# The product of attention weights and v: f32 exponentials as moving operand for even heads, f16 pairs for odd heads

## The chip, the cores and the metric

One core of one Trainium2 chip runs the whole program in one launch. The metric is the device time in microseconds (us), the median of several runs. Engines are named as the profile names them: PE (TensorE matmuls), PEld (its weight loads), DVE (VectorE), ACT (ScalarE), POOL (GpSimd), SP (the engine whose queue issues the loads here).

## The reference, cut to what matters

```python
# q, k, v: (2, 8, 768, 64) f32; centroids: (8, 16, 64)
q_assign = argmax(einsum('bhsd,hcd->bhsc', q_n, c_n)); k_assign likewise
mask   = q_assign[:, :, :, None] == k_assign[:, :, None, :]
scores = where(mask, q @ k.T / 8, -1e9);  scores -= max(scores)
attn   = exp(scores);  attn = attn / (sum(attn) + 1e-9)
x      = (attn @ v)                   # the product that is changed
x      = moe(x)                       # x @ w_in, an activation, @ w_out
out    = moe2(x)                      # 8 experts, Sinkhorn-balanced gates
```

There are 16 heads (2 x 8) of 768 queries, 768 keys and 64 columns of v. A query whose cluster holds no key has all its scores at -1e9, so its row is the mean of all v; the kernel calls this case "absorbed" by the tables `Wt`.

## The kernel before, in words

Everything that must be exact to f32 is done on PE with f16 pairs: a value is split into a high f16 part and the f16 rest, and a product takes three matmuls (high x high, high x rest, rest x high), each at the f16 pace.

Attention (L395 to L975) is a hand-written software pipeline. A **unit** is one head and one tile of 128 keys, so a head has `NJ` = 6 units, the stage has `NU` = 96, and a pair of heads, which shares its preparation, has 12. The loop at L952 counts steps `g`; in step `g` the engines' queues get, in this order:

- `max_unit` for unit `g + 8` (L659): two matmuls of 384 columns into `pmt`, the one PSUM tile of its kind, and one DVE reduction of 768 columns (L675) that finds the row maxima. The next `max_unit` can only write `pmt` when this reduction is done.
- `e_split` for unit `g - 1` (L732): the exponentials `E`, f32, are cast to `Eh` (f16) on ACT (L740), or on DVE (L738) for 3 units of 12; then POOL forms the rest `El = E - Eh` in two halves of 384 columns (L742).
- `s_mm` for unit `g` (L711): four matmuls of 384 columns (L721, L725) give the scores of 128 keys against 768 queries, and one ACT instruction takes the exponentials of 768 columns (L729).
- `pv_mm` for unit `g - LAG`, `LAG` = 4 (L745): `Eh` and `El` are the stationary operands, six tiles of 128 queries each, and v the moving one, 64 or 65 columns (the 65th is a column of ones that sums the weights). That is 6 x 2 matmuls with `Eh` (v's high and rest part) and 6 with `El`: 18 in a unit, and 12 more with `Wt` in the last unit of a head (L766 to L770). The result has queries on the partitions.
- the tasks that `PLACE`, `PLAN2`, `PLANV` (L470, L929, L930) and the loops at L940 to L951 give to this step, woven with a few DVE chains (`weave`, L695): the preparation of later pairs of heads (loads, scaling, f16 splits of q and k, cluster argmax, DMA transposes by SP), the f16 pair of v (`vhi` on ACT L522, `vlo` on DVE L527), the tables `Wt` (`abs1` on PE L613, `abs2` on DVE L623 to L641), the decoding of the first MoE weights (`w00`, L187 to L205, L380, L383), and the evacuation of finished heads (`evac_tasks`, L774: DVE L787 to L789, ACT L794, POOL L797, and for odd heads the DMA transposes into `xT` L800).

All engine queues are in order, so a step that waits holds up all behind it on its engine. PSUM has 8 banks: `pmt` takes 2, the score tiles `ps_s` 2 x 2, and `ps_v` (`pv`, `abs`, `sim`, `red`) 2. When the last units have run, PE goes on with the first MoE layer (`l1_mm`, L898), of which two groups are put among the last two attention steps.

Of the kernel before, what the change touches and what calls it, by code (L numbers as in the profile page):

```python
# [8 lines left out]
F32 = mybir.dt.float32  # L9
# [9 lines left out]
P = 128  # L19
# [12 lines left out]
def attention_moe_kernel(  # L32
# [39 lines left out]
    one = const.tile([P, 1], F32, name="one")  # L72

# [327 lines left out]
    ps_s = actx.enter_context(tc.tile_pool(name="ps_s", bufs=2, space=PSUM))  # L401
    ps_v = actx.enter_context(tc.tile_pool(name="ps_v", bufs=2, space=PSUM))
# [6 lines left out]
    Wt = [ap1.tile([P, 2, 130], F16, name=f"Wt{i}") for i in range(2)]  # L409
# [60 lines left out]
    PLACE = [-34, -31, -28, -28, -27, -26, -25, -25, -24, -24, -23, -19, -18, -17, -16, -15, -14, -14, -21, -19, -11, -9, -9]  # L470

    def prep_tasks(p, parts=None):
# [134 lines left out]
        def abs1():  # L607

            ps = ps_v.tile([P, 2, 256], F32, tag="v", name=f"abs{p}")
            for h in range(2):  # L610
                for j in range(NJ):
                    t = h * NJ + j
                    nc.tensor.matmul(  # L613
                        ps[:, h, 0:129], lhsT=ka[:, t, :], rhs=d["vn"][:, t, 0:129],
                        start=(j == 0), stop=(j == NJ - 1))
            d["ab"] = ps

        def abs2():
# [3 lines left out]

            def hi(h):  # L623
                nc.vector.tensor_scalar(
                    out=w[r, h, 0:D + 1], in0=ps[r, h, 0:D + 1], scalar1=c[r, h:h + 1], scalar2=None, op0=ALU.mult)

            def rest(h):
                nc.vector.scalar_tensor_tensor(
                    out=t[r, h], in0=ps[r, h, 0:D], scalar=c[r, h:h + 1], in1=w[r, h, 0:D],
                    op0=ALU.mult, op1=ALU.subtract)  # L630

            def lo(h):
                nc.vector.scalar_tensor_tensor(
                    out=w[r, h, D + 1:129], in0=ps[r, h, D + 1:129], scalar=c[r, h:h + 1], in1=t[r, h],
                    op0=ALU.mult, op1=ALU.add)
# [23 lines left out]
    def max_unit(i, j):  # L659
# [7 lines left out]
        ps = ps_s.tile([P, 2, 512], F32, tag="s", name=f"pm{i}_{j}") if early else pmt  # L667
# [41 lines left out]
    pvt = {}  # L709

    def s_mm(i, c):  # L711

        p, hh = divmod(i, 2)
        d = st[p]
        ps = ps_s.tile([P, 2, 512], F32, tag="s", name=f"pS{i}_{c}")
# [4 lines left out]
        for g in range(2):  # L720
            nc.tensor.matmul(  # L721
                ps[:, g, 0:N2], lhsT=d["kB"][:, t, :], rhs=qb[:, hh * S + g * N2:hh * S + (g + 1) * N2],
                start=True, stop=False)
        for g in range(2):
            nc.tensor.matmul(  # L725
                ps[:, g, 0:N2], lhsT=d["kA"][0:KR, t, :], rhs=qa[0:KR, g * N2:(g + 1) * N2],
                start=False, stop=True)
        E = ap2.tile([P, 2, N2], F32, tag="E", name=f"E{i}_{c}", bufs=3)
        nc.scalar.activation(E, ps[:, :, 0:N2], AF.Exp, scale=d["esc"][:, 0:1])  # L729
        EE[i, c] = E  # L730

    def e_split(i, c):  # L732
        E = EE.pop((i, c))
        Eh = ap3.tile([P, 2, N2], F16, tag="Eh", name=f"Eh{i}_{c}", bufs=5)
        El = ap3.tile([P, 2, N2], F16, tag="El", name=f"El{i}_{c}", bufs=5)
        n = NJ * i + c
        if n % 12 in (0, 3, 5) or n >= NU - LEAD and n % 2:
            nc.vector.tensor_copy(Eh, E)  # L738
        else:
            nc.scalar.copy(Eh, E)  # L740
        for g in range(2):
            nc.gpsimd.tensor_tensor(out=El[:, g], in0=E[:, g], in1=Eh[:, g], op=ALU.subtract)  # L742
        EE[i, c] = (Eh, El)
# [899 lines left out]
```

## Time and profile before

| | |
|---|---|
| median of 3 runs | 1530.16 us (1527.67 to 1531.33) |
| the profiled execution, span from first to last instruction | 1526.7 us |
| busy in the span: PE, PEld, DVE, ACT, POOL | 1418.7, 764.8, 955.4, 665.3, 387.8 us |
| mean granted PE clock | 0.974 of 2.4 GHz |
| attention's exponentials, first to last start | 39.5 to 288.7 us |
| last matmul of the product with v | 296.9 us |

The profiled execution gives its span alone; what lies around it (launch and end) is in the runs' times. The median is 3.5 us above this span. Attention is the first fifth of the program; behind it come the two MoE parts, in which PE is busy throughout. The change touches attention alone, so the rows below are almost all of this stage. A time per unit is a stretch's length by the number of its exponentials; a busy time by the same number is the work that an engine has per unit.

### The profile page before, as it was taken

What the parts mean: (1) busy time and instruction counts of PE and PEld (TensorE: products, weight loads), DVE (VectorE), ACT (ScalarE), POOL (GpSimd) and SP (SyncE); (2) the same over time, 40 slices, a digit from 0 to 9 for tenths busy, and PEclk for the clock granted to TensorE, in tenths of its full rate; (3) what the DMA queues carried; (4) which work ended last, traced back from release to release, by engine and by line L of the source; (5) the groups of instructions that cost most, each with busy time, mean ns of one, the idle gap of its engine ahead of it and who ended that gap; (6) DMA issues with size and microseconds to landing.
All of it is one profiled execution on the core that took longest, in us unless ns stands there. A gap on an engine that the chain in (4) does not pass through costs nothing.

```text
span 1526.7 us, 22967 instructions
## 1 busy us (share of the span) xinstructions
PE 1418.7 (93%) x9289; PEld 764.8 (50%) x9289; DVE 955.4 (63%) x1732; ACT 665.3 (44%) x1123; POOL 387.8 (25%) x427
## 2 busy tenths in 40 slices
PE   3878888898999998999999999999999999999998
PEld 1555556543444444544555555555555555555554
DVE  7889898876756866466565466466456565564333
ACT  2677777475553444343344333333333333324221
POOL 1579889752101321030030020020020020021000
PEclk9799899898999998999999999999999999999999
DMA  9675743331321100101101101101101101100011
GB/s 217 145 162 102 134 87 62 91 116 52 129 69 56 56 0 1 55 1 56 56 1 55 56 1 56 56 1 56 55 1 55 56 1 55 38 19 1 1 42 42
DMA packets 106633, 87.60 MB, mean 57 GB/s; under 512 B 78368, under 2 KB 88608, under 8 KB 106528
## 3 DMA queue, kind: packets, MB, share of 16 engines
q1 hardware_dynamic: 106528, 86.15, 20.8%
q8 instruction: 72, 1.18, 0.3%
q14 instruction: 33, 0.27, 0.1%
HBM read 64.01 MB, written 3.15 MB: 44 GB/s over the span
## 4 chain that ended last, share of the span: by engine, by line
PE 71%; DVE 17%; ACT 5%; issue 4%; DMA 1%; POOL 0%; DVEq 0%; ACTq 0%; POOLq 0%; SPq 0%
PE o L1471 11%; PE o L1472 11%; PE o L1470 11%; PE X L1521 5%; PE X L1524 5%; PE X L1523 5%; PE Y L1521 4%; PE Y L1524 4%; PE Y L1523 4%; DVE pmt L675 3%; PE l L1248 2%; PE pmt L672 1%; PE l L912 1%; PE l L913 1%; PE l L914 1%
## 5 line engine op out<-in xcount | busy, mean ns | idle before, releaser
L1472 PE MATMUL o<-w_s,hl 128*128 128x512 f16 x768 | 291.6, 380 | 0.0
L1471 PE MATMUL o<-w_s,hh 128*128 128x512 f16 x768 | 291.5, 380 | 0.0
L1470 PE MATMUL o<-w_s,hh 128*128 128x512 f16 x768 | 291.3, 379 | 0.0
L1540 ACT ACTIVATE hh<-u 128x384 f16<-128x384 f32 x192 | 100.3, 522 | 374.9 <-DVE u L1536 374.9
L742 POOL TENSOR_TENSOR El<-E,Eh 128x384 f16<-128x384 f32 x192 | 189.3, 1014 | 72.8 <-DVE Eh L738 41.2
L1541 DVE SCALAR_TENSOR_TENSOR hl<-u,hh 128x384 f16<-128x384 f32 x192 | 112.8, 587 | 120.1 <-ACT hh L1540 120.1
L1536 DVE TENSOR_TENSOR u<-X,snap 128x384 f32<-128x384 f32 x64 | 35.7, 557 | 189.5 <-PE X L1524 189.5
L121 POOL PARTITION_ALL_REDUCE w_m<-w_mx x14 | 5.4, 383 | 570.2 <-DVE w_mx L1336 332.7
L1523 PEld LDWEIGHTS <-wop 128*128 128x128 f16 x896 | 87.9, 98 | 93.6 <-issue 13.5
L1521 PEld LDWEIGHTS <-wop 128*128 128x128 f16 x896 | 87.9, 98 | 81.9 <-issue 1.1
L1536 DVE TENSOR_TENSOR u<-Y,snap 128x384 f32<-128x384 f32 x128 | 70.8, 553 | 80.1 <-PE Y L1524 79.1
L1472 PEld LDWEIGHTS <-hl 128*128 128x128 f16 x768 | 75.2, 98 | 90.8 <-issue 0.3
L1248 PE MATMUL l<-hh,w_s 128*128 128x512 f16 x384 | 118.3, 379 | 0.0
L1524 PEld LDWEIGHTS <-wop 128*128 128x128 f16 x896 | 87.9, 98 | 58.5 <-issue 0.9
L729 ACT ACTIVATE E<-pS,esc 128x768 f32<-128x768 f32 x96 | 86.2, 900 | 65.7 <-PE pS L725 48.4
L1470 PEld LDWEIGHTS <-hh 128*128 128x128 f16 x768 | 76.0, 99 | 66.5 <-issue 0.2
L1529 ACT COPY snap<-X 128x384 f32<-128x384 f32 x128 | 61.2, 478 | 109.7 <-PE X L1524 108.3
L1471 PEld LDWEIGHTS <-hh 128*128 128x128 f16 x768 | 75.2, 98 | 66.5 <-issue 0.2
L675 DVE TENSOR_REDUCE pmt<-pmt 128x1 f32<-128x768 f32 x84 | 80.6, 960 | 19.5 <-PE pmt L672 18.7
L672 PE MATMUL pmt<-kA,qA 80*128 80x384 f16 x184 | 52.1, 369 | 42.5 <-DVE pmt L675 14.2
L1248 PEld LDWEIGHTS <-w_s 128*128 128x128 f16 x576 | 56.4, 98 | 67.5
L1521 PE MATMUL X<-xop,wop 128*128 128x384 f16 x256 | 83.8, 327 | 6.8 <-ACT snap L1529 5.5
(280 smaller groups left out, 2990.5 us busy)
## 6 DMA issues: line engine op xcount, KB each, us to landing
w_raw<-in_moe_w_dram SPq DMA_DIRECT2D x16, 2048.0 KB, 8.2
w_c<-in_moe_w_out_dram SPq DMA_DIRECT2D x16, 512.0 KB, 3.5
w00x<-in_moe_w_in_dram SPq DMA_DIRECT2D x8, 512.0 KB, 5.6
w00f<-in_moe_w_in_dram SPq DMA_DIRECT2D x8, 512.0 KB, 4.1
w_c<-in_moe_w_in_dram SPq DMA_DIRECT2D x8, 512.0 KB, 3.8
qraw<-in_q_dram SPq DMA_DIRECT2D x8, 384.0 KB, 3.8
kraw<-in_k_dram SPq DMA_DIRECT2D x8, 384.0 KB, 4.8
vraw<-in_v_dram SPq DMA_DIRECT2D x2, 1536.0 KB, 10.6
```

The lines of the kernel that those rows point to most:

```text
L675: nc.vector.tensor_reduce(nmx[i][:, j:j + 1], ps[:, :, 0:N2], axis=AX.XY, op=ALU.max, negate=True)
L742: nc.gpsimd.tensor_tensor(out=El[:, g], in0=E[:, g], in1=Eh[:, g], op=ALU.subtract)
L1248: nc.tensor.matmul(po[i], lhsT=a, rhs=r, start=(f == 0 and z == 0), stop=(f == NFC - 1 and z == 2))
L1470: nc.tensor.matmul(pe2[t], lhsT=a, rhs=wh, start=first, stop=False)
L1471: nc.tensor.matmul(pe2[t], lhsT=a, rhs=wl, start=False, stop=False)
L1472: nc.tensor.matmul(pe2[t], lhsT=b, rhs=wh, start=False, stop=last)
L1521: nc.tensor.matmul(o[:, 0:XT], lhsT=wh, rhs=xh, start=(first and c == 0), stop=False, skip_group_check=True)
L1523: nc.tensor.matmul(o[:, 0:XT], lhsT=wh, rhs=xl, start=False, stop=False, skip_group_check=True)
L1524: nc.tensor.matmul(o[:, 0:XT], lhsT=wl, rhs=xh, start=False, stop=(c == 1), skip_group_check=True)
L1536: nc.vector.tensor_tensor(h, src, r[k], op=ALU.add)
L1540: nc.scalar.activation(hh, src, AF.Relu)
L1541: nc.vector.scalar_tensor_tensor(out=hl, in0=src, scalar=0.0, in1=hh, op0=ALU.max, op1=ALU.subtract)
```

## The change

For heads 0, 2, 4, ... the product is turned round. The f32 exponentials are the moving operand (two halves of 384 queries) and v, in f32 with two columns of ones, is the stationary one (66 columns); the result `pvT` has v's columns on the partitions, is copied to SBUF by ACT and turned back by three PE transposes for each half. No `Eh`, no `El` and no f16 pair of v is made for these heads. For heads 1, 3, 5, ... (`SPLIT`) the product is as before, with the casts all on ACT. Scores and exponentials come in halves of 384 queries, with three one-bank score tiles; `ps_v` has three banks. The product lags by 3 units instead of 4. v is scaled to f32 once; `vlo` on DVE goes, and POOL makes column sums of v and, for odd heads, the f16 rest (ACT the f16 copy). The tables `Wt` come from one f32 matmul with ones and 12 matmuls of one column, and five DVE instructions a pair instead of seven. The v tasks stand 8 to 5 steps ahead of their pair instead of 21 to 9.

```diff
-    ps_s = actx.enter_context(tc.tile_pool(name="ps_s", bufs=2, space=PSUM))
-    ps_v = actx.enter_context(tc.tile_pool(name="ps_v", bufs=2, space=PSUM))
+    ps_v = actx.enter_context(tc.tile_pool(name="ps_v", bufs=3, space=PSUM))
...
+    DW = D + 2
+    SPLIT = tuple(range(1, NHEAD, 2))
...
-    PLACE = [-34, -31, ..., -14, -14, -21, -19, -11, -9, -9]
+    PLACE = [-34, -31, ..., -14, -14, -8, -7, -6, -5, -5]
...
         def vhi():
-            vn = d["vn"] = ap3.tile([P, 2 * NJ, 130], F16, tag="vn", name=f"vn{p}")
+            vn = d["vn"] = ap2.tile([P, 2 * NJ, DW], F32, tag="vn", name=f"vn{p}")
             nc.scalar.activation(vn[:, :, 0:D], vr, AF.Copy, scale=sv[0][:, 0:1])
-        def vlo():
-            nc.vector.scalar_tensor_tensor(
-                out=vn[:, :, D + 1:2 * D + 1], in0=vr, scalar=sv[0][:, 0:1], in1=vn[:, :, 0:D],
+        def vsum():
+            nc.gpsimd.tensor_tensor(out=t, in0=vn[:, :, 0:3], in1=vn[:, :, 3:6], op=ALU.add)
+            nc.gpsimd.tensor_tensor(out=t[:, :, 0], in0=t[:, :, 0], in1=t[:, :, 1], op=ALU.add)
+            nc.gpsimd.tensor_tensor(out=t[:, :, 0], in0=t[:, :, 0], in1=t[:, :, 2], op=ALU.add)
+            for hh in range(2):
+                if 2 * p + hh in SPLIT:
+                    nc.scalar.copy(x[:, :, 0:D + 1], v[:, :, 0:D + 1])
+                    nc.gpsimd.tensor_tensor(
+                        out=x[:, :, D + 1:2 * D + 1], in0=v[:, :, 0:D], in1=x[:, :, 0:D], op=ALU.subtract)
...
-    def s_mm(i, c):
+    def s_mm(h):
+        ps = ps_s.tile([P, N2], F32, tag="s", name=f"pS{h}")
+        nc.tensor.matmul(ps, lhsT=d["kB"][:, t, :], rhs=qb[...], start=True, stop=False)
+        nc.tensor.matmul(ps, lhsT=d["kA"][0:KR, t, :], rhs=qa[...], start=False, stop=True)
+        E = ap2.tile([P, N2], F32, tag="E", name=f"E{h}", bufs=8)
+        nc.scalar.activation(E, ps, AF.Exp, scale=d["esc"][:, 0:1])
+    def e_split(h):
+        if h // (2 * NJ) not in SPLIT:
+            return
+        nc.scalar.copy(Eh, E)
+        nc.gpsimd.tensor_tensor(out=El, in0=E, in1=Eh, op=ALU.subtract)
+    def pv_mm(h):
...
+        ps = pvT[i, g][0:DW]
+        nc.tensor.matmul(ps, lhsT=d["vn"][:, hh * NJ + c, :], rhs=E, start=(c == 0), stop=False)
+        if c == NJ - 1:
+            nc.tensor.matmul(ps, lhsT=W[:, 0:DW], rhs=q, start=False, stop=False)
+            nc.tensor.matmul(ps, lhsT=W[:, DW:2 * DW], rhs=q, start=False, stop=True)
+    def turn_tasks(i, g):
+            nc.scalar.copy(o[0:DW], pvT.pop((i, g))[0:DW])
+            for n in range(NJ // 2):
+                nc.tensor.matmul(
+                    pvt[i][:, 3 * g + n, :], lhsT=x["o"][0:DW, P * n:P * n + P], rhs=ident[0:DW, 0:DW],
+                    is_transpose=True, start=(g == 0 and n == 0), stop=True, skip_group_check=True)
...
-    LAG = 4
+    LAG = 3
+    TURN = 2
+        for z in range(2):
+            if 0 <= g < NU:
+                s_mm(2 * g + z)
+            if 0 <= 2 * g + z - 1 < 2 * NU:
+                e_split(2 * g + z - 1)
+            if 0 <= gp < NU:
+                pv_mm(2 * gp + z)
```

## Rows read from the trace of the kernel before

**Rows 1.** Busy time of each engine (x instructions), six stretches from 39.4 us on
```profile
core 0: us, PE busy (x) PEld busy (x) DVE busy (x) ACT busy (x) POOL busy (x), PEclk, DMA share, GB/s
39.40:110.90 71.50, 57.32 (x680) 39.20 (x679) 58.48 (x115) 46.83 (x65) 48.37 (x54) 0.83 0.66 149
110.90:170.00 59.10, 47.48 (x738) 34.48 (x737) 54.99 (x95) 46.58 (x65) 53.90 (x58) 0.98 0.66 127
170.00:204.30 34.30, 29.05 (x399) 21.26 (x397) 29.64 (x59) 24.16 (x35) 27.97 (x29) 0.83 0.47 85
204.30:234.00 29.70, 23.32 (x357) 17.03 (x355) 27.30 (x45) 21.82 (x30) 27.96 (x29) 0.94 0.52 97
234.00:288.80 54.80, 46.29 (x656) 33.90 (x652) 44.96 (x65) 38.79 (x52) 51.04 (x52) 0.84 0.35 70
288.80:297.00 8.20, 6.60 (x88) 4.11 (x89) 6.43 (x6) 3.09 (x5) 7.58 (x7) 1.00 0.02 5
```
**Rows 2.** The same view, exponentials (L729) alone: ACT busy and their count
```profile
110.90:170.00 59.10, 21.38 (x24) 0.98 0.66 127
```
**Rows 3.** Groups of instructions by line, 39 to 298 us
```profile
L742 POOL TENSOR_TENSOR El<-E,Eh 128x384 f16<-128x384 f32 x192 | 189.3, 1014 | 72.8 <-DVE Eh L738 41.2 <-issue 14.2 <-DVE x_r L787 9.4
L729 ACT ACTIVATE E<-pS,esc 128x768 f32<-128x768 f32 x96 | 86.2, 900 | 65.7 <-PE pS L725 48.4 <-POOL El L742 10.1 <-DVE ab L628 2.2
L675 DVE TENSOR_REDUCE pmt<-pmt 128x1 f32<-128x768 f32 x84 | 80.6, 960 | 19.5 <-PE pmt L672 18.7
L740 ACT CAST Eh<-E 128x768 f16<-128x768 f32 x69 | 57.1, 828 | 1.4
L738 DVE CAST Eh<-E 128x768 f16<-128x768 f32 x27 | 23.0, 853 | 3.4 <-ACT E L729 3.2
L527 DVE SCALAR_TENSOR_TENSOR vn<-vraw,v_s,vn 128x768 f16<-128x768 f32 x8 | 10.0, 1248 | 0.0
L565 PE MATMUL sim<-CT,qB 128*128 128x16 f16 x72 | 4.3, 169 | 0.3 <-DVE x_f L789 0.3
L628 DVE SCALAR_TENSOR_TENSOR ab<-abs,ab_c,Wt 16x64 f32<-16x64 f32 x16 | 4.5, 281 | 0.6
L794 ACT CAST xn<-x_f 128x384 f16<-128x384 f32 x15 | 7.5, 501 | 0.0
```
**Rows 4.** Timeline of PE from 161.7 us: start, busy, tile, count
```profile
161.71 0.48 PE L672 MATMUL pmt<-kA,qA 80*128 80x384 f16 x2
162.03 0.49 PE L721 MATMUL pS<-qB,kB 128*128 128x384 f16 x2
162.68 0.54 PE L757 MATMUL pv<-vn,Eh 128*128 128x65 f16 x12
163.06 0.34 PE L757 MATMUL pv<-vn,El 128*128 128x65 f16 x6
163.24 0.54 PE L757 MATMUL pv<-Wt,qA 80*128 80x65 f16 x12
```
**Rows 5.** Instructions of L76 and L86, f32 operands: ns min/median/max, first and last start
```profile
L76 PE MATMUL red<-ident,pad x15: 272/306/475, 6.3 to 533.7; 128*128 128x128 f32 x15
L86 PE MATMUL red<-ident,qk_r x16: 251/312/374, 7.2 to 197.0; 128*128 128x2 f32 x16
```
**Rows 6.** The page's costliest groups: ACT reading 384 columns of PSUM
```profile
L1529 ACT COPY snap<-X 128x384 f32<-128x384 f32 x128 | 61.2, 478 | 109.7 <-PE X L1524 108.3
```
**Rows 7.** Timeline of DVE, the same decode beside POOL's subtractions and after them
```profile
294.32 1.29 DVE L205 SCALAR_TENSOR_TENSOR w00t<-w00f,w00t 128x512 uint32<-128x512 uint32 x1
...
304.65 0.69 DVE L205 SCALAR_TENSOR_TENSOR w00t<-w00f,w00t 128x512 uint32<-128x512 uint32 x1
```
**Rows 8.** Timeline, the last POOL subtractions and the last exponential
```profile
279.25 13.44 POOL L742 TENSOR_TENSOR El<-E,Eh 128x384 f16<-128x384 f32 x12
...
288.74 0.90 ACT L729 ACTIVATE E<-pS,esc 128x768 f32<-128x768 f32 x1 [0.30 <-POOL El L742]
```
**Rows 9.** Timeline of PE in a stretch at half clock
```profile
62.86 0.80 PE L672 MATMUL pmt<-kA,qA 80*128 80x384 f16 x2 [0.92 <-DVE pmt L675]
63.45 0.85 PE L721 MATMUL pS<-qB,kB 128*128 128x384 f16 x2
64.09 0.85 PE L725 MATMUL pS<-qA,kA 82*128 82x384 f16 x2
```

More of the change, by code (lines that the diff above doesn't have):

```diff
@@ L621, in abs2 @@
             t = ap2.tile([P, 2, D], F32, tag="ab", name=f"ab{p}", bufs=1)
[L623 to L635, printed above, removed]
+            none = -float(S) * MASK
             return [
+                lambda: nc.vector.tensor_single_scalar(c[r], ps[r, :, D], none, op=ALU.is_equal),
                 lambda: nc.vector.tensor_scalar(
-                    out=c[r], in0=ps[r, :, D], scalar1=-float(S) * MASK, scalar2=-1.0 / MASK,
+                    out=w[r, :, D], in0=ps[r, :, D], scalar1=none, scalar2=float(S),
                     op0=ALU.is_equal, op1=ALU.mult),
-            ] + [lambda g=g, h=h: g(h) for g in (hi, rest, lo) for h in range(2)]
+                lambda: nc.vector.tensor_tensor(
+                    t[r], ps[r, :, 0:D], c[r].unsqueeze(2).to_broadcast([C, 2, D]), op=ALU.mult),
+                lambda: nc.vector.tensor_copy(w[r, :, 0:D], t[r]),
+                lambda: nc.vector.tensor_tensor(w[r, :, DW:DW + D], t[r], w[r, :, 0:D], op=ALU.subtract),
+            ]
         def abs2_first():
-            d["abs"] = abs2()
-            return d["abs"][:3]
+            return abs2()
         def abs3():
-            return d.pop("abs")[3:]
+            return []
         first = [squares(0, qr), squares(1, kr), scale0, scale1, scale2]
-        last = [vhi, vlo, abs1, abs2_first, abs3]
+        last = [vhi, vsum, abs1, abs2_first, abs3]
         if parts:
@@ L666, in max_unit @@
         early = NJ * i + j < LEAD and j % 2
-        ps = ps_s.tile([P, 2, 512], F32, tag="s", name=f"pm{i}_{j}") if early else pmt
+        ps = ps_s.tile([P, 2, 512], F32, tag="pm", name=f"pm{i}_{j}") if early else pmt
         t = hh * NJ + j
@@ L719, in s_mm @@
         qa = d[f"qA2_{hh}"].rearrange("p a b -> p (a b)")
[L720 to L743, printed above, removed]
@@ L759, in pv_mm @@
[L759 to L770 removed]
+        E = EE.pop(h)
@@ new lines, in pv_mm, with acc @@
+        qa = d[f"qA2_{hh}"]
+        W = Wt[p % 2][0:D + C, hh]
+        if i in SPLIT:
+            if x == 0:
+                pvt[i] = ps_v.tile([P, NJ, DW], F32, tag="v", name=f"pv{i}")
+            ps = pvt[i]
+            Eh, El = E
+            vn = d["v16", hh][:, c, :]
+            vs = vn[:, 0:D + 1], vn[:, D + 1:2 * D + 1]
+            def acc(j, w, r, **kw):
+                kw = {"start": False, "stop": False, **kw}
+                nc.tensor.matmul(ps[:, j, 0:r.shape[1]], lhsT=w, rhs=r, skip_group_check=True, **kw)
+            for n in range(NJ // 2):
+                w = Eh[:, P * n:P * n + P]
+                acc(3 * g + n, w, vs[0], start=(x == 0 and n == 0))
+                acc(3 * g + n, w, vs[1])
+            for n in range(NJ // 2):
+                acc(3 * g + n, El[:, P * n:P * n + P], vs[0])
+            if x == 2 * NJ - 1:
+                for j in range(NJ):
+                    w = qa[0:D + C, j, :]
+                    acc(j, w, W[:, 0:D + 1])
+                    acc(j, w, W[:, DW:DW + D], stop=(j == NJ - 1))
+            return
@@ new lines, in turn_tasks, with t0, t1 @@
+    def turn_tasks(i, g):
+        x = {}
+        def t0():
+            o = x["o"] = ap2.tile([P, N2], F32, tag="oT", name=f"oT{i}_{g}")
+            nc.scalar.copy(o[0:DW], pvT.pop((i, g))[0:DW])
+        def t1():
+            if g == 0:
+                pvt[i] = ps_v.tile([P, NJ, DW], F32, tag="v", name=f"pv{i}")
+            for n in range(NJ // 2):
+                nc.tensor.matmul(
+                    pvt[i][:, 3 * g + n, :], lhsT=x["o"][0:DW, P * n:P * n + P], rhs=ident[0:DW, 0:DW],
+                    is_transpose=True, start=(g == 0 and n == 0), stop=True, skip_group_check=True)
+        return [t0, t1]
```

98 lines of the change are left out of this document (56 added, 42 removed).

## The prediction
> **What bounds the kernel now.** I read the busy times by stretch first, because the change lives in one stage. Attention's units run from 39.4 to 297.0 us. In the regular middle 24 units take 59.1 us, 2.46 us each [rows 1, 2]. There DVE is busy 54.99 of 59.1 us and POOL 53.90, so each has some 2.25 us of work in a unit and idles under a tenth; ACT has 46.58 (1.94 a unit). PE's 47.48 overstates its work, since its records overlap. By starts, two 384-column matmuls take 0.32 us (161.71 to 162.03, two `pmt` before two scores), the next four 0.65 us, the 18 pairs of the product 0.56 us (162.68 to 163.24) [rows 4]: 1.53 us a unit, and about 0.16 more for some 60 short matmuls a pair of heads at the same 31 ns. So PE has 1.7 us of work in 2.46; DVE and POOL bound the middle, coupled through in-order queues.
>
> Next the groups by line: POOL's work is almost only `El`, 192 x 1.014 us; DVE's largest term is the max reduction, 0.960 us a unit, and the change's own terms are the casts, 27 x 0.853, and `vlo`, 8 x 1.248 [rows 3]. Third, one DVE instruction at two times: a decode takes 1.29 us beside POOL's subtractions and 0.69 us after them [rows 7]. POOL's work lengthens DVE's. Last the end: the last exponential starts at 288.74, the product ends 8 us later, behind POOL's backlog of 12 subtractions in 13.44 us [rows 1, 8]. PE then goes straight on with the MoE layer, so what the stage gains or loses passes to the total.
>
> **The change part by part.** POOL: half the subtractions go, 96 x 1.014 = 97 us. It gets about 2.7 us a pair of heads for sums and the f16 rest of v (two 384-column operations at 1.0, two smaller ones at my estimate of 0.35), 22 us in all. POOL stays near 2.3 us a unit in odd heads and falls under 0.6 in even ones.
>
> DVE: casts 23.0 and `vlo` 10.0 us go; the tables' seven instructions become five, two a pair saved at 0.281, some 4.5 us. That is 38 us of 222, or 0.39 us a unit: 2.25 becomes about 1.86, and less where POOL rests.
>
> ACT: an exponential of 768 columns (0.900) becomes two of 384. The nearest rows are 0.478 (a 384-column copy out of PSUM [rows 6]) and 0.501 (a cast from SBUF [rows 3]); half of 0.900 is the lower bound, 0.55 my upper one (0.05 above the dearer row, for the function). I take 0.48, the row with the same source: +0.06 a unit. Odd heads cast both halves on ACT, 2 x 0.50. Other ACT work, 46.58 less 24 exponentials and some 17 casts at 0.83, is under 0.5 a unit. Even units get 0.96 + 0.45 + 0.16 (two result copies a head) = 1.6, odd ones 0.96 + 1.0 + 0.45 = 2.4, less some overlap: 2.35.
>
> PE, even heads: the 18 pairs (0.56) become two f32 matmuls of 384 moving columns. The trace has no wide f32 matmul. An ordinary f32 matmul leaves two records (16 for the eight calls with `qk_r`), a transposing one leaves one; that one, 128 columns, takes 272 ns at least and 306 in the median [rows 5] against 169 for 16 f16 columns [rows 3]. Less the fixed part of 162 (169 without sixteen columns at 0.42 ns), it costs 0.86 to 1.12 ns a column, where f16 costs 0.42. If each record of an ordinary one costs the same, a half takes 2 x 384 x 0.86 = 0.66 to 0.86 us; the lower end is two records at the f16 pace, 2 x 0.16 = 0.32. I take 0.66, the cleanest record of the nearest form: 1.32 a unit. The weight load I set at nothing: the previous matmul, over 0.3 us long, covers it; uncovered it would add 0.1 to 0.2 us a half. Per head come four f16 matmuls with `Wt` (0.65) and six transposes (estimate 0.1 each, up to 0.27). An even unit then has 0.32 + 0.65 + 1.32 + 0.11 + 0.10 + 0.2 = **2.7 us of PE work**; the short matmuls of a pair's similarities fall into these steps.
>
> The Trainium skill speaks against the cheap end: "FP8 and Floating Point Precision", section TensorE Precision Notes, has true f32 as four passes through the array. An estimate from it is 4 x 0.16 = 0.64 us a half, which agrees with the transposing row; with the cheap end instead, the stage would win 48 x 0.68 = 33 us more of PE room.
>
> Steps and waits: in a pair's 12 steps, the f32 products fall on steps 3 to 8 (lag 3), the ACT-heavy casts on 6 to 11. Steps 3 to 8 are set by PE: 2.7, and 2.8 with the waits for `pmt` that stay. Steps 9 to 11 are set by ACT, 2.35, with POOL beside it at 2.3. Steps 0 to 2 have light PE, ACT and POOL, so DVE sets them: about 2.0, or 2.1 where the weight decode falls, now at its undisturbed pace. A pair takes 6 x 2.8 + 3 x 2.35 + 3 x 2.05 = 30.0 us; the last two, without later pairs' preparation, 29.
>
> New waits: the turn's transposes wait for ACT's copy, a step earlier in its queue; behind them on PE stand the next maxima and scores. With a step of 2.8 us between I cost that at nothing; an uncovered wait would cost up to one exponential and cast, 1 us a half, 16 us in all. The tables come later but still three steps ahead of use. The v sums enter POOL's queue at step 5, when it is idle. Loads and DMA transposes keep their order; SP gets nothing new, and the even heads' evacuation, two steps later, issues no DMA. The shorter lag saves one unit at the end, and POOL has no backlog there: of the 8.2 us tail I keep 5.
>
> Sum: pairs 0 and 1, slowed by DVE and half clock, 71.5 to 65 (half of the pair's excess over the middle, since their DVE work shrinks but scans and slow clock stay); pairs 2 and 3, 59.1 to 60; pair 4, 34.3 to 30.5; pair 5, 29.7 to 30.5; pairs 6 and 7 (25 units), 54.8 to 59; tail 8.2 to 5. The stage goes from 257.6 to 250, **-8 us**. The profiled span becomes 1518.7; the median is 3.5 us above the span, which I carry over: **1522 us**.
>
> The clock: two score matmuls take 0.64 us in a half-clock stretch (1.2 GHz, 63.45 to 64.09) after a gap of 0.92 us [rows 9], and the granted clock is 0.83 to 0.98 [rows 1]. An f32 unit at half clock would cost over 4.5 us. Since denser PE work leaves fewer such gaps, I assume full clock there; this is the softest assumption.
>
> **Rivals.** (a) Slower: even units starve PE. DVE and POOL reach nine tenths of their pace today; if PE, now the bound, reaches only 85%, an f32 unit takes 2.7 / 0.85 = 3.15, and 48 x 0.35 = +17 less my 8 gives +9, 1539. It decides from 2.97 a unit on (48 x 0.17 = 8). For it: one `pmt` tile and in-order waits, half-clock stretches; against: DVE and POOL have slack in just these steps. Chance 0.25.
>
> (b) ACT binds: half exponentials at 0.55 and casts at 0.50 give odd units 2.6 or more in six steps of twelve (the last three of PE's included); 24 units x 0.3 is +7, 1529. For it: both instructions pay their fixed cost twice; against: ACT's overlap of successive instructions. Chance 0.12.
>
> (c) More gain: f32 units reach 2.7 and the others 2.1, as DVE's relief by a quiet POOL spreads: 48 x 0.1 + 24 x 0.25 + 2 = 13 more, 1509. For it: 0.69 against 1.29 [rows 7]. Chance 0.16.
>
> (d) Weight loads set PE's pace in the f16 pairs. Then f32 would relieve PE instead of loading it: 18 loads one after another, at 0.1 us, take 1.8 us a unit against 1.32, and 48 x 0.48 = 23 us would be won beyond the rest: 1499. Against it the 18 pairs in 0.56 us [rows 4]. Chance 0.03. The Trainium skill, "TensorE: Matmul & The Clock Gate", section LDWEIGHTS, would have it so: a load takes its columns by 1.2 in ns, 107 for 128. As a pace this trace does not bear it out.
>
> **How the numbers follow.** The forecast, 1514 to 1530, has 0.42; 0.02 is for what I have not seen. The range is 1506 to 1540: it takes in (b), (c) and most of (a); (d) and a still dearer f32 matmul (0.86 a half, +19 us) stay outside. A measurement here tells 0.2%, about 3 us, from no change. Faster: most of the forecast, (c), (d): 0.56. Same: the forecast's edge and half of (b): 0.13. Slower: (a), the rest of (b), uncovered waits: 0.31.
>
> **What would show it.** Right: f32 matmuls with two records each, a half's pace near 0.66 us; units of 2.7 to 2.9 in steps 3 to 8 with PE hardly idle; POOL some 75 us less busy and DVE near 185 us in the stage; the decode at 0.7 us more often; exponentials near 0.48. Wrong: f32 units over 3.0 with PE waiting for `pmt`, for a score tile or for the turn's copy; a half-clock stretch inside the f32 steps; ACT without idle time in odd heads; or all steps alike, which would mean that the phases even out in the buffers.

## The result, and the profile after

The changed kernel takes **1545.89 us** (median of 4 runs, 1544.97 to 1548.38) against 1530.74 for the kernel before in the same runs: ratio 1.0095, 95% interval 1.0074 to 1.0117. It is slower by some 15 us, outside the range and on the other side of the forecast. The profiled span is 1544.7 us (before 1526.7, +18.0). Both spans are of one execution each, and that of the kernel before is one of its faster ones, so they lie further apart than the medians. Attention's last product matmul ends 15.8 us later than before (312.9 against 297.1): its first exponential starts 1.3 us later (40.77 against 39.50), and from there the stage takes 272.1 us instead of 257.6.

Line numbers here are those of the changed kernel: L728 and L730 scores, L733 exponential, L742 and L743 the cast and rest of odd heads, L764 the f16 product, L781 the f32 product, L792 the copy of the transposed result, L798 its turn, L624 the tables' matmul, L506 the first operation of a pair's scale, L945 the next layer. An experiment that adds lines shifts them by a few.

The groups by line of the changed kernel, 39 to 313 us (busy time, mean ns of one, idle time before and what ended it); they answer to [rows 3, 7]:

```profile
L733 ACT ACTIVATE E<-pS,esc 128x384 f32<-128x384 f32 x192 | 110.2, 583 | 78.1 <-PE pS L730 75.1 <-POOL El L743 2.2
L743 POOL TENSOR_TENSOR El<-E,Eh 128x384 f16<-128x384 f32 x96 | 88.5, 933 | 63.5 <-ACT Eh L742 43.2 <-PE pS L730 6.3 <-issue 6.1
L681 DVE TENSOR_REDUCE pmt<-pmt 128x1 f32<-128x768 f32 x84 | 80.9, 964 | 70.0 <-PE pmt L678 69.6
L781 PE MATMUL pvT<-E,vn 128*66 128x384 f32 x192 | 78.7, 491 | 0.4 <-ACT vn L526 0.4
...
L206 DVE SCALAR_TENSOR_TENSOR w00t<-w00f,w00t 128x512 uint32<-128x512 uint32 x6 | 4.2, 693 | 0.2
```

What was to be removed is removed: the rests fall from 189.3 to 88.5 us on POOL, and a decode on DVE takes 0.693 us where it took up to 1.29 [rows 7]. But the engines relieved now stand idle for TensorE: the max reduction waits 69.6 us for it where it waited 18.7 [rows 3], the exponential 75.1 us where it waited 48.4. TensorE, busy 236.3 of the stage's 272.1 us, is now the fullest engine, so what counts is how it spends a pair. Windows of the changed kernel, pairs 2, 3 and 4 from one pair's first exponential to the next:

```profile
core 0: us, PE busy (x) PEld busy (x) DVE busy (x) ACT busy (x) POOL busy (x), PEclk, DMA share, GB/s
120.84:154.91 34.07, 29.36 (x292) 18.05 (x292) 22.16 (x43) 24.36 (x52) 17.03 (x22) 0.95 0.49 93
154.91:188.95 34.04, 29.35 (x293) 18.19 (x293) 21.13 (x41) 24.34 (x51) 17.19 (x22) 0.95 0.57 125
188.95:227.08 38.13, 33.07 (x291) 20.27 (x291) 25.52 (x53) 25.61 (x54) 18.19 (x22) 0.82 0.38 77
```

In pairs 2 and 3 TensorE is busy 29.4 of 34 us, with 4.7 us idle and a granted clock under 1. Its largest waits, 37 to 313 us, name what the forecast had no line for:

```profile
PE pv L764 <- DVE qk_e L506: 8.0, 5, 1.8
PE pmt L678 <- DVE pmt L681: 6.7, 7, 1.7
PE pmt L678 <- DVE a_oh L603: 4.0, 5, 3.1
PE abs L624 <- ACT oT L792: 3.5, 4, 0.9
```

The first and the last of these lines are odd at sight. An odd head's product has no use for the scale of a later pair, nor the tables for the copy of a transposed product. What they share is `ps_v`, the pool of three PSUM tiles. The odd head's product takes, at step 9 of a pair, the tile in which `red` stands until VectorE's scale has read it; the tables' matmul takes, at step 6, the tile of `pvT`'s first half, whose copy to SBUF is queued on ScalarE in the same step. In both cases the other two tiles are still held by the program's order: at step 9 by `pvT`'s second half, whose copy starts only at 182.91 us in pair 3, and by the turned result; at step 6 by the similarities `sim` and by `pvT`'s second half itself. TensorE's timeline in pair 3 shows an undisturbed f32 unit and then both waits:

```profile
160.41 0.49 PE L678 MATMUL pmt<-kA,qA 80*128 80x384 f16 x2
...
161.06 0.81 PE L781 MATMUL pvT<-E,vn 128*66 128x384 f32 x2
161.71 0.32 PE L728 MATMUL pS<-qB,kB 128*128 128x384 f16 x1
...
162.68 0.49 PE L678 MATMUL pmt<-kA,qA 80*128 80x384 f16 x2
...
172.09 0.46 PE L624 MATMUL abs<-vs,one 128*128 128x128 f32 x2 [0.89 <-ACT oT L792]
...
181.22 0.35 PE L764 MATMUL pv<-v,Eh 128*128 128x65 f16 x6 [1.52 <-DVE qk_e L506]
```

On VectorE, the scale that frees the tile stands behind a maximum's reduction, its row operations and one of the similarities' operations, though the product has been due since 179.70 (181.22 less its wait of 1.52):

```profile
179.41 0.97 DVE L681 TENSOR_REDUCE pmt<-pmt 128x1 f32<-128x768 f32 x1 [0.82 <-PE pmt L678]
...
180.49 0.54 DVE L599 TENSOR_REDUCE a_cm<-a_eq 128x24 f16<-128x384 f16 x1
...
181.02 0.15 DVE L506 TENSOR_SCALAR qk_e<-red 128x2 int32<-128x2 int32 x1
```

The length of the pairs, between the starts of the first exponentials in the timelines (us; the last column but one to the last exponential, the last from there to the end of the product):

| kernel | pairs 0, 1 | 2, 3 | 4 | 5 | 6, 7 | tail |
|---|---|---|---|---|---|---|
| before | 74.3 | 59.6 | 33.8 | 28.9 | 52.7 | 8.3 |
| changed | 80.1 | 68.1 | 38.1 | 31.0 | 49.8 | 5.1 |
| e12 (below) | 77.9 | 61.6 | 33.9 | 29.7 | 49.8 | 5.6 |

The loss is in the pairs in whose steps a later pair is prepared; the last two, without preparation, are 2.9 us shorter than before.

### The profile page after: what moved, and what is told of

Its sections match the earlier page's. It is cut to its first block, busy times and chain, and to the rows that moved or that the text cites. A ratio compares the mean times of both kernels' runs of the same rounds, so it can differ in the third digit from the quotient of the medians.

```text
span 1544.7 us, 21682 instructions
## 1 busy us (share of the span) xinstructions
PE 1446.5 (94%) x8617; PEld 758.1 (49%) x8617; DVE 913.1 (59%) x1681; ACT 676.9 (44%) x1270; POOL 310.7 (20%) x364
## 3 DMA queue, kind: packets, MB, share of 16 engines
HBM read 64.01 MB, written 3.15 MB: 43 GB/s over the span
## 4 chain that ended last, share of the span: by engine, by line
PE 65%; DVE 8%; ACT 4%; issue 2%; DMA 1%; SPq 0%; POOL 0%; DVEq 0%; ACTq 0%; POOLq 0%
PE o L1525 10%; PE o L1526 10%; PE o L1524 10%; PE X L1575 5%; PE X L1578 5%; PE X L1577 5%; PE Y L1575 4%; PE Y L1577 4%; PE Y L1578 4%; PE l L1302 2%; PE l L945 1%; PE l L946 1%; PE l L947 1%; DVE w_raw L206 1%; DVE w_t L204 1%
## 5 line engine op out<-in xcount | busy, mean ns | idle before, releaser
L733 ACT ACTIVATE E<-pS,esc 128x384 f32<-128x384 f32 x192 | 110.2, 583 | 78.1 <-PE pS L730 75.1
L681 DVE TENSOR_REDUCE pmt<-pmt 128x1 f32<-128x768 f32 x84 | 80.9, 964 | 70.0 <-PE pmt L678 69.6
L743 POOL TENSOR_TENSOR El<-E,Eh 128x384 f16<-128x384 f32 x96 | 88.5, 933 | 63.5 <-ACT Eh L742 43.2
L1575 PE MATMUL X<-xT,wop 128*128 128x384 f16 x256 | 83.4, 326 | 1.3 <-DVE lg_r L82 1.3
```

The lines of the kernel that those rows point to most:

```text
L733: nc.scalar.activation(E, ps, AF.Exp, scale=d["esc"][:, 0:1])
L743: nc.gpsimd.tensor_tensor(out=El, in0=E, in1=Eh, op=ALU.subtract)
L1575: nc.tensor.matmul(o[:, 0:XT], lhsT=wh, rhs=xh, start=(first and c == 0), stop=False, skip_group_check=True)
```

## The experiments

**e1: less TensorE work in the even heads.** One f16 matmul a half in place of the f32 one; ScalarE makes one more copy of v a pair for it, and v's f32 tile has one buffer instead of two. All else is as changed. The cut:

```
         E = ap2.tile([P, N2], F32, tag="E", name=f"E{h}", bufs=8)
+        if i not in SPLIT:
+            E = E.bitcast(F16)[:, 0:N2]
...
-        nc.tensor.matmul(ps, lhsT=d["vn"][:, hh * NJ + c, :], rhs=E, ...)
+        nc.tensor.matmul(ps, lhsT=d["v16", hh][:, c, :], rhs=E, ...)
```

> The changed kernel, but in even heads the exponentials are written in f16 and v is taken in f16 (both rests are left out), so the turned product is one f16 matmul of 384 columns instead of an f32 one: some 0.16 us a half instead of 0.65, 0.98 us less PE work in each of 48 units. Theory A (in the steps of the f32 product PE has no idle time, 18.5 us for the six units of a head in the middle pairs, and the stage's loss is made there): these steps fall to about 13.5 us, where ACT and DVE have 12.5 and 10.5 us of work; 1505 to 1515 us. Theory B (the loss is in waits on PE's queue: PSUM tiles, the max tile, the shorter lag): the time stays within 5 us of the changed kernel's 1546.

Measured: 1549.76 us, ratio to the kernel before 1.0121 (1.0096 to 1.0146): no gain at all. Its three largest waits, 37 to 313 us, and the window of 173 to 190 us:

```profile
PE pmt L680 <- DVE pmt L683: 9.7, 12, 1.7
PE abs L626 <- ACT oT L796: 7.8, 4, 2.4
PE pv L768 <- DVE qk_e L506: 6.5, 5, 1.5
```

```profile
173.00:190.00 17.00, 14.95 (x91) 8.85 (x92) 9.69 (x20) 8.60 (x20) 7.46 (x10) 0.51 0.34 90
```

A TensorE that is early waits longer at the tables (7.8 us instead of 3.5) and for the maxima (9.7 instead of 6.7), at the product somewhat less (6.5 instead of 8.0). And from 173 us, where a wait of 1.95 us for the tables' tile ends, it runs 17 us at a granted clock of 0.51 (the lower of its two levels, 1.2 GHz). So the amount of f32 work alone is not the loss.

**e2: the two tiles free when they are asked for.** Two places in the order of preparation moved: the scale one step earlier, the tables' matmuls and what follows them one step later.

```
-    PLACE = [..., -28, -28, -27, -26, ..., -8, -7, -6, -5, -5]
+    PLACE = [..., -28, -28, -28, -26, ..., -8, -7, -5, -4, -4]
```

> The changed kernel with two waits for PSUM tiles of the product's pool taken out by moving prepared tasks by one step: the scale of q and k is formed a step earlier (so that the odd head's first product finds its tile, 1.5 us each in 5 pairs) and the tables' matmuls come a step later, behind the copy of the first half (0.9 us each in 4 pairs). Theory A (PE work in the f32 steps is the loss): 5 to 11 us won, since PE is without slack and a wait taken away is PE time; 1535 to 1541. Theory B (the waits are the loss): the whole 15 us, 1531 or under. If neither wait is on the path: 1545.

Measured: 1531.72 us, ratio 1.0013 (1.0000 to 1.0026). Against the kernel before in the same runs (1529.80) 1.9 us of the 15.2 are left, so 13 are back. Neither wait is left in its trace under its name, though the matmuls of the maxima now wait 7.3 us over seven for VectorE's row operations (L696), where the changed kernel had 0.9.

**e5 and e6: each move by itself.**

> One of the two moves of e2 alone: scale2 at -28, the tables where the change has them. Tile theory (the loss is TensorE's two waits for PSUM product tiles and the half clock behind them): the wait of the odd head's first product (8.0 us over five in the changed kernel) goes, the tables' wait (3.5 us over four) stays; in proportion to the two, 9 to 10 of e2's 14 us come back, about 1536 us. Rival, that one wait is as bad as the other because either brings on the half clock: about 7 us, 1539. Rival, that e2's gain came from the tables: 1543 to 1546.

> The other move of e2 alone: the tables' steps at -5, -4, -4, scale2 at -27. Tile theory: the tables' wait (3.5 us over four) goes, the product's wait (8.0 over five) stays: 4 to 5 us come back, about 1541. Rival, either wait is as bad as the other: about 1539. Rival, the gain was the scale's: 1544 to 1546. If the two together give more than the sum of each alone, a wait that stays takes over what the other gave up.

Measured: e5 1538.08 us (1.0045, 1.0032 to 1.0059), e6 1541.86 us (1.0071, 1.0058 to 1.0085). Each against the kernel before in its own runs, they win back 7.4 and 3.6 us, 11.0 of e2's 13.2: nearly a sum, and about in the proportion of the two waits (8.0 and 3.5). In each trace the other wait stays at its size (3.6 us over four in e5, 8.4 over five in e6). The 2.2 us that only both moves give no run explains.

**e12: one more tile, not an instruction moved.** The moves of e2 also change what stands in VectorE's and ScalarE's steps. This takes the shortage away by itself.

```
-    ps_v = actx.enter_context(tc.tile_pool(name="ps_v", bufs=3, space=PSUM))
+    ps_v = actx.enter_context(tc.tile_pool(name="ps_v", bufs=4, space=PSUM))
-            ps_s = actx.enter_context(tc.tile_pool(name="ps_s", bufs=3, space=PSUM))
+            ps_s = actx.enter_context(tc.tile_pool(name="ps_s", bufs=2, space=PSUM))
```

> The changed kernel with its own order and one PSUM tile more for products (four), one less for scores (two). Tile theory: the odd head's product no longer waits for the scale's tile (8.0 us over five), nor the tables for the transposed product's (3.5 over four), though not an instruction moved; if the third score tile is worth little the time falls as far as e2's, 1530 to 1536; TensorE waiting for ScalarE at the scores would say how much of it that tile costs. Rival, e2 gained by easing VectorE's and ScalarE's steps and not by the tiles: TensorE waits in the same places under other names, 1542 to 1549.

Measured: 1532.46 us, ratio 1.0007 (0.9995 to 1.0020), 1.0 us over the kernel before in the same runs: 14 of the 15 us are back. Waits of e12, 37 to 300 us, and its windows, pairs 2, 3 and 4:

```profile
PE pmt L678 <- DVE a_oh L603: 4.9, 5, 1.2
PE pmt L678 <- DVE pmt L681: 4.4, 6, 1.4
PE pmt L678 <- DVE a_eq L595: 3.8, 2, 3.2
PE pmt L678 <- DVE qk_e L506: 3.4, 5, 0.9
...
PE pS L728 <- ACT E L733: 0.9, 3, 0.3
```

```profile
117.19:147.87 30.68, 27.60 (x292) 17.48 (x292) 22.65 (x43) 24.34 (x52) 17.01 (x22) 1.00 0.56 104
147.87:178.74 30.87, 27.66 (x293) 17.55 (x293) 21.65 (x41) 24.32 (x51) 17.20 (x22) 1.00 0.65 129
178.74:212.63 33.89, 29.05 (x291) 18.22 (x291) 26.00 (x53) 25.50 (x54) 18.15 (x22) 0.95 0.54 94
```

Neither the product nor the tables wait any more; the score tile given up costs 0.9 us of waiting. The rival has a part all the same: with the product through, the next maximum's matmul waits for the same scale (`qk_e`), 3.4 us of the 8.0. Against the changed kernel's windows, pair 2 with the same 292 matmuls loses 1.6 us of idle time (4.71 to 3.08) and 1.8 us of *busy* time (29.36 to 27.60), as its clock goes from 0.95 to 1.00. The whole stage, from the first exponential to the last product matmul, says the same, the changed kernel first and then e12:

```profile
40.77:312.91 272.14, 236.31 (x2230) 143.27 (x2228) 177.33 (x330) 191.45 (x392) 134.45 (x162) 0.94 0.48 102
39.26:297.65 258.39, 229.65 (x2230) 140.72 (x2228) 180.73 (x330) 191.77 (x393) 134.27 (x162) 0.97 0.52 107
```

With 2230 matmuls in both, TensorE is idle 7.1 us less (35.8 to 28.7) and busy 6.7 us less: about half of the price is idle time and half the lower clock.

In pairs 2 and 3 the lower clock does not stand right behind the two waits (in pairs 0 and 4 the product's wait, to 71.07 and 218.04 us, does end in it). Pair 3 by steps, in us between the starts of the maxima's matmuls (L678) on TensorE, from 151.87 us in the changed kernel, 144.71 in e2 and 145.64 in e12:

| | steps 0 to 2 | 3 to 8 (f32) | 9 to 11 | pair |
|---|---|---|---|---|
| forecast | 6.15 | 16.8 | 7.05 | 30.0 |
| changed | 8.5 | 18.5 | 7.1 | 34.1 |
| e2 | 7.1 | 17.4 | 6.4 | 31.0 |
| e12 | 6.6 | 17.2 | 7.2 | 31.0 |

The tables' wait costs where it stands, in step 6 (3.9 us, in e12 2.8). The product's wait, in step 9, makes steps 9 to 11 no longer than in e12, where the next maximum waits for the same scale. But steps 0 to 2, here of the changed kernel and then of e2, run at another clock:

```profile
151.87:160.41 8.54, 6.89 (x87) 4.90 (x85) 5.67 (x9) 6.93 (x14) 5.76 (x8) 0.80 0.66 124
144.71:151.85 7.14, 5.32 (x87) 3.92 (x85) 5.67 (x9) 6.57 (x14) 5.10 (x7) 1.00 0.61 114
```

The same 87 matmuls take 6.89 us instead of 5.32, with no more idle time (1.65 and 1.82 us); each stretch holds one long wait for `pmt`, of 1.65 and 1.53 us. From 112 to 226 us, in e5 (the product's wait gone) and then in e6 (the tables' wait gone):

```profile
112.00:226.00 114.00, 96.07 (x1008) 59.43 (x1008) 80.40 (x156) 85.65 (x176) 59.84 (x72) 1.00 0.57 108
112.00:226.00 114.00, 100.60 (x983) 63.41 (x981) 74.82 (x145) 83.87 (x173) 58.38 (x70) 0.89 0.51 99
```

So the lower clock of these pairs goes with the product's wait, some steps behind it. How the one brings on the other no run here isolates.

**e3 and e4: without the f32 product, first attempt.** e3 swaps even and odd heads; e4 gives every head f16 pairs. Both change `SPLIT` and make the f16 pairs of v for the heads concerned.

> The changed kernel with the roles of even and odd heads exchanged: f32 product for odd heads, so the f32 steps fall on steps 9 to 2 of a pair, where no similarities (1.2 us of short matmuls) and no tables stand on PE. Theory A: the f32 steps get shorter by the 2 us of these matmuls and the f16 steps take them into PE's idle time, some 2 us in six pairs, less 2 to 3 us for the last head, whose result must be turned before the MoE layer can have it: 1535 to 1541. Theory B: the waits only move, 1543 to 1550. If DVE, which has most of its preparation on steps 9 to 2, binds there with PE: no gain either, and PE waits for the max reduction in the f32 steps.

> The changed kernel with f16 pairs for all heads: no f32 product and no turn, but all the rest of the change (exponentials and scores in halves, casts all on ACT, lag of three units, three score tiles of one bank, sums of v, the new places). Theory A: without the f32 steps PE has idle time again; ACT (two exponentials and two casts, 2.0 us a unit with their overlap, and 0.45 of other work) and POOL (2.0 and 0.3) bind at 2.45 to 2.6 us a unit, so 1528 to 1542. Theory B (the parts other than the f32 product cost the 15 us): 1546 or more, and slower than the changed kernel by what POOL and ACT add.

Measured: e3 1562.60 us (1.0201, 1.0176 to 1.0226), e4 1571.13 us (1.0259, 1.0238 to 1.0279). Neither answers its question: a new wait decides. Of e3:

```profile
PE abs L627 <- POOL vs L543: 24.6, 8, 4.8
```

With even heads' rests ahead of them in its queue, POOL makes v's sums late, and TensorE waits at the tables (25.3 us over eight in e4). In the changed kernel the sums come when POOL has no rests; that placing is part of what makes it work.

**e7: less TensorE work once the two waits are gone.** e1's edit with e2's order; as in e1 the rests of the even heads are left out.

> Both moves of e2, and the even heads' exponentials and v as one f16 value, one matmul a half (the rests of the even heads are left out). TensorE theory (with the two waits gone the pairs are bound by TensorE, busy 27.6 of 30.7 us a pair in e2): twelve halves a pair at some 0.16 in place of 0.65 us take 5.8 us off TensorE, the pair falls to what ScalarE needs (24.2 busy, with gaps some 27), and six pairs give about 18 us: 1510 to 1518. Rival, that relief of TensorE is paid back at half clock as in e1: 1527 to 1534.

Measured: 1525.75 us, ratio 0.9969 (0.9956 to 0.9981). That is 6 us under e2, between the two expectations. Windows of e7, pairs 3 and 4:

```profile
149.80:177.58 27.78, 22.57 (x281) 15.37 (x281) 19.93 (x41) 24.10 (x53) 17.11 (x22) 1.00 0.69 152
177.58:210.83 33.25, 28.14 (x279) 17.98 (x279) 25.60 (x53) 25.59 (x55) 18.42 (x22) 0.79 0.45 88
```

Pair 3, at full clock throughout, has 5.1 us less TensorE work than in e12 (22.57 against 27.66) and is 3.1 us shorter; pair 4 runs at 0.79 and is busy 28.1 us with less work. So TensorE's work does count in e2 and e12, but part of its relief comes back as half clock. No single engine is full in e7; what sets its 28 us is not shown.

**e8 and e10: half of each even head in f16 pairs.** The first 384 queries in f32 and turned, the rest as in odd heads; e10 has the tables' steps of e9.

```
-        if h // (2 * NJ) not in SPLIT:
+        if h // (2 * NJ) not in SPLIT and h % (2 * NJ) < NJ:
...
-        if i in SPLIT:
+        if i in SPLIT or g == 1:
```

> Both moves of e2, and of every even head only the first half of its queries in f32 (turned back), the second half in f16 pairs like the odd heads, with the pairs of v made for both heads. A pair then has TensorE at about 27.6 - 6 x (0.65 - 0.28) - turns = 25.1 us, ScalarE at 24.2 + 6 x 0.5 + 0.5 - 0.6 = 27.3, GpSimd at 17 + 6 x 0.93 + 0.6 = 23.2. TensorE theory: pairs shrink by 2 us of 30.7, five or six of them: 1519 to 1523. ScalarE rival: its casts take the place of TensorE, no gain over e2: 1529 to 1534.

> e8 with the tables' steps where e9 has them. e8 came out 17 us over e2 with TensorE waiting 10.7 us over four for the sums that stand behind the rests on GpSimd. If that wait was its loss: TensorE 25.1 us a pair, ScalarE 27.3, GpSimd 23.2, so 2 us a pair under e9, 1517 to 1524. Rival, ScalarE with its added casts sets the pairs: at e9's time or up to 8 us over it.

Measured: e8 1548.40 us (1.0106, 1.0086 to 1.0126), with TensorE waiting 10.7 us over four for the sums, as in e3. e10 1540.79 us (1.0067, 1.0049 to 1.0085), still with 9.8 us of that wait over three: as much as the 9.3 us by which it is slower than e9, so neither run prices ScalarE's added casts.

**e9: the tables' steps where VectorE and POOL are free.**

```
-    PLACE = [..., -28, -28, -27, -26, ..., -14, -14, -8, -7, -6, -5, -5]
+    PLACE = [..., -28, -28, -28, -26, ..., -14, -14, -11, -10, -8, -7, -7]
```

> scale2 at -28 as in e2, and the whole of the tables earlier: v's scaling -11, its sums -10, their product -8, the table's VectorE part -7, in steps in which VectorE has nothing else and no rest of an odd head stands ahead of the sums on GpSimd. Tile theory: neither of the two waits, as in e2; and the step that holds the scale loses five VectorE operations, so the matmuls of the maxima wait less for VectorE (7.5, 7.3 and 5.4 us in e2's three groups): 1522 to 1529. Rival, that the waits for VectorE are the price of any order with 27.6 us of TensorE work in 30.7: as e2, 1530 to 1533.

Measured: 1531.48 us, ratio 1.0002 (0.9993 to 1.0012): as e2 within the intervals. This second order without either wait is worth no more.

**e11: every head in f16 pairs, with e9's order.**

> Every head in f16 pairs with the rest of the change kept (casts on ScalarE, rests on GpSimd, the lag of three), and the tables where e9 has them: what the f32 product itself is worth. TensorE falls to some 24 us a pair, ScalarE rises by 12 casts of 0.5 us less four copies to about 28, GpSimd by 12 rests of 0.93 to 28. If TensorE's f32 work is what holds e9's pairs at 30: about e9 less 6, near 1520. Rival, ScalarE and GpSimd take its place, so the f32 product is worth having: e9 plus 5 to 20 us, 1533 to 1550.

Measured: 1552.34 us, ratio 1.0144 (1.0124 to 1.0164), 2 us beyond the rival's range. Windows from the first exponential of pair 2 on, e9 and then e11 (to the last exponential in e9, to one three units from the end in e11):

```profile
115.77:289.89 174.12, 157.64 (x1610) 98.66 (x1610) 119.77 (x226) 136.70 (x285) 98.81 (x116) 0.99 0.47 95
```

```profile
125.88:305.46 179.58, 140.94 (x2073) 102.54 (x2070) 133.52 (x222) 155.58 (x339) 162.50 (x186) 0.90 0.47 90
```

Without f32, TensorE has less to do and POOL (162.5 of 179.6) and ScalarE (155.6) fill instead. With the rest of the change and these places kept, the f32 product is worth 21 us (1552.34 against 1531.48). But 14.6 us of the sums' wait are in this price and a lower clock (0.90 against 0.99), so it is not the price of the f16 pairs' work alone. Giving the f32 product up at these places makes the kernel slower, not faster.

**e13 to e16: behind attention.** In e9 attention ends 2.1 us before that of the kernel before (1.1 of them because its first exponential starts earlier, at 38.38 us), and the span is 2.8 us longer. The first matmuls of the next layer's third block, in the kernel before and then in e9:

```profile
296.54 0.54 PE L757 MATMUL pv<-Wt,qA 80*128 80x65 f16 x12
296.91 0.38 PE L912 MATMUL l<-xT,w_s 128*128 128x512 f16 x1
```

```profile
294.45 0.53 PE L764 MATMUL pv<-Wt,qA 80*128 80x65 f16 x12
297.88 0.61 PE L945 MATMUL l<-xT,w_s 128*128 128x512 f16 x1 [2.89 <-DVE x_f L821]
298.27 0.63 PE L946 MATMUL l<-xT,w_s 128*128 128x512 f16 x1
298.70 0.63 PE L947 MATMUL l<-xT,w_s 128*128 128x512 f16 x1
```

A third wait of the same kind: the change opens `ps_v` before `ps_s`, so the layer's third block gets a bank in which the last head's product still stands, where before it got one of the scores'. Then the block starts at half clock (0.43 us a matmul, 0.215 before). e13 and e14 give that block a score bank, in the changed kernel and in e9; e15 adds e12's fourth tile; e16 adds to e14 an earlier start of the decodes that VectorE still has behind attention.

```
-    for n, g in (("ps_b", (2, 3, 6, 7)), ("ps_c", (4, 5))):
+    for n, g in (("ps_b", (2, 3, 4)), ("ps_c", (6, 7, 5))):
...
-        u = 48 + 12 * c if c < 4 else 89 + 6 * (c - 4)
+        u = 48 + 10 * c if c < 4 else 86 + 5 * (c - 4)
```

> The changed kernel with one line: the pools of the layer behind attention named in another order, so that the third block of its first matmuls takes a bank that held scores, not the one that held the last head's product. In the changed kernel, and in every kernel with its pools, that block waits 2.9 us for VectorE to read the last product and then runs at half clock (0.43 us a matmul in place of 0.215 for some 5.5 us in e9). In the kernel before, the scores' pool lay first and the block went straight on. Third-wait theory: 5 us come back, 1540 to 1542. Rival, the layer behind is bound by VectorE's decodes and takes the time back: 1544 to 1547.

> e9 with that line. e9's attention ends 2 us before that of the kernel before and its span is 2.8 us longer; if the third wait and its half clock are the whole of that, 5 us come back: 1525 to 1528, which is below the kernel before. Rival, the decodes behind attention bind: 1529 to 1532.

> e14 with four product tiles and two score tiles. If some waits for product tiles are left in e14's order: a few us less, 1522 to 1526. Rival, the third score tile is worth more in that order: e14 plus 1 to 4.

> e14 with the decodes of the first expert's columns (five VectorE operations each) begun earlier, the last at step 101 in place of 107, into steps where VectorE now waits for TensorE. If the time VectorE gained in attention can be spent so: TensorE's wait for a maximum behind the first blocks (3.0 us in e9) goes, 1522 to 1526. Rival, the decodes stand ahead of maxima that TensorE waits for, and give it back inside attention: 1526 to 1532.

Measured: e13 1545.42 us (1.0098, 1.0082 to 1.0115), e14 1530.42 (1.0004, 0.9991 to 1.0016), e15 1530.44 (1.0000, 0.9987 to 1.0013), e16 1531.73 (1.0010, 1.0000 to 1.0020). The wait is gone from e13 and e14 and the time hardly falls. Much of what is won goes into the next wait for VectorE's decodes, here in e9, in e14 and, as L76, in the kernel before:

```profile
346.66 0.30 PE L77 MATMUL red<-ident,pad 128*128 128x128 f32 x1 [3.04 <-DVE pad L101]
```

```profile
344.10 0.45 PE L77 MATMUL red<-ident,pad 128*128 128x128 f32 x1 [5.70 <-DVE pad L101]
```

```profile
344.27 0.45 PE L76 MATMUL red<-ident,pad 128*128 128x128 f32 x1 [4.46 <-DVE pad L100]
```

TensorE comes to this matmul 5.2 us earlier in e14 than in e9 and runs it 2.6 us earlier; the wait takes the other 2.7. And though e14's attention ends 2.1 us before that of the kernel before, the two are level here (344.10 and 344.27). So the rival holds as far as this wait: behind attention VectorE binds, and TensorE's time won there is waited away. Of the 2.6 us by which e14 is still ahead of e9 the ratios show nothing (1.0004 and 1.0002), and no run shows where they go.

In e16 this wait is down to 2.5 us, but attention ends later (the last exponential starts at 296.37, in e14 at 289.86). The expected reason, maxima that wait for the decodes, is not what the traces show: TensorE is idle 28.9 us in the stage (28.7 in e14) and busy 233.8 with the same 2231 matmuls (227.6), at a granted clock of 0.94 (0.97). In these two executions the loss is nearly all clock.

No version here that keeps the whole computation beats the kernel before; e2, e9, e12, e14, e15 and e16 come within 2 us of it.

## Why the prediction was wrong

**The step that failed** is the part on waits. It took the waits that stay at 0.1 us a unit and looked for new ones only at the turn's copy, as a matter of that copy's readers, at a price of nothing. For the tables it asked when they are used, not which tile they are formed in. The PSUM tiles of `ps_v` were not followed at all, though the diff shows the pool and the new users: in even heads two half-head tiles and one for the turned result instead of one, a step earlier by the shorter lag, beside `sim`, `red` and `abs`. The tables' matmul and the odd product each need a tile that an in-order queue elsewhere frees in the same step: 3.5 and 8.0 us of waits. Shown by e12: one more tile, and 14 of the 15 us are back. That the prediction's price of uncovered waits at the turn, 16 us, is near this loss is luck: it was for another place, and was left out of the sum.

**The clock**, called the softest assumption, failed with it, at another place than the one in doubt: in pairs 2 to 4 the f32 matmuls run at full clock, but in pair 3 steps 0 to 2 do not (0.80), and over the stage that is as much as the idle time (6.7 and 7.1 us). The forecast's row for it was misread, too. The half-clock stretch of [rows 9] was there before the gap of 0.92 us that it was tied to: the granted clock is 0.50 already from 60.00 to 62.80 us, behind a wait of 1.76 us that ended at 57.97.

**Rival (a)** named the sign and nearly the price (1539): TensorE, now the fullest engine, is busy 29.4 of 34 us, 86% where the rival said 85. In-order waits and half-clock stretches were among its reasons, the tiles were not. Its place was half right: in pair 3 the f32 units take 3.08 us each (3.15 by the rival, 2.8 by the forecast), but that is 1.7 of the pair's excess of 4.1 us, and 2.4 are in steps 0 to 2.

**With the waits gone** the stage is 0.8 us longer than before (258.4 in e12 against 257.6), not 8 shorter. By the table: pairs 0 and 1 were to shrink by 6.5 us and grew by 3.6; pair 4 was to shrink by 3.8 and stayed; pairs 6 and 7 were to grow by 4.2 and shrank by 2.9. The first two were priced by VectorE's relief. In pairs 0 and 1 its work did fall, from 61.0 of 74.3 us to 53.9 of 77.9, but TensorE's rose from 60.0 to 64.6. I would argue that the stretch follows TensorE; no run here separates it from the waits of these pairs. Why the last two shrank, no run shows either; I would argue that without preparation POOL was their limit before. Which part of the change keeps the stage from its forecast once the tiles suffice stays open; e7 puts the part of the f32 work at some 6 us.

**What passes to the total**: the forecast let the stage's difference through one to one. Behind attention a third tile wait and VectorE's decodes take back 2.0 us (e14) to 4.5 us (e9) of what attention has won, up to VectorE's wait at 344 to 347 us.

**Terms, by size.** f32 half: forecast 0.66 us, measured 0.65 (161.06 to 161.71), two records each. The Trainium skill, "FP8 and Floating Point Precision", section TensorE Precision Notes, has four passes for f32, by which the estimate was 0.64 us; the trace agrees. The load of f32 weights costs nothing beside it, as forecast: TensorE idles 0.4 us ahead of all 192. Six f32 steps: 16.8 us forecast, 18.5 measured in pair 3 (160.41 to 178.88); an undisturbed unit is 2.28 us, and the products with `Wt`, similarities, tables, turns, the scale's two matmuls and 1.3 us of waits make the rest. Exponential half: 0.583 us, not 0.48 and above the upper bound of 0.55; the row of a plain copy was too cheap, but ScalarE does not bind here (25 of 34 us busy in a pair), so rival (b) did not come. VectorE: 177.3 us in the stage (185 forecast). POOL: 134.5 against 216.8, 82 less (75). Tail: 5.1 us (5).

## What to carry to other kernels

When a change adds tiles to a small PSUM pool or moves their uses, list for each step which tile is taken, who frees it, and what stands ahead of that instruction in its queue; a wait that pairs two unrelated names in the trace can be such a tile. Where one engine becomes the bound, relief elsewhere may be worth nothing until that engine's own waits are gone. Look for what TensorE's waits cost in its busy time as well as in its idle time, and not only right behind them: here about half of the price was a lower clock, in pairs 2 and 3 some steps later. Try one more buffer at the price of another pool's before rearranging steps: it tells at once whether a tile is short.

## What was not expected of the hardware

ScalarE's exponential of 384 columns from PSUM takes 583 ns where a copy of the same size takes 478 [rows 6] (66 partitions: 474, L792), while 768 columns take 900 [rows 3]: the halves cost 0.27 us more a unit. An f32 matmul of 384 columns runs at 0.65 us with two records whose mean is 491 ns, so records of one pair overlap. And with 1.6 us of idle time removed in a pair, the matmuls get faster: busy time falls 1.8 us at equal count, as the granted clock goes from 0.95 to 1.00.
